# Issuing v and block 1's q first, and giving the last projection's halves a PSUM buffer each

## Chip, cores and metric

The kernel runs on one core of one Trainium2 chip. The metric is the device time of one execution in microseconds, as the median of several runs. Engines are named as in the profile: PE (TensorE, with PEld for its weight loads), DVE (VectorE), ACT (ScalarE), POOL (GpSimd) and SP (SyncE, which only issues transfers here).

## What is computed

Chunk-selected attention followed by an RMS norm and a SwiGLU feed-forward network, all from float32 inputs to a float32 output of 3072 x 512:

```python
# q, k, v: (4 batches, 8 heads, 768 tokens, 64)
k_min, k_max = k_chunks.min(3), k_chunks.max(3)            # chunks of 32 tokens
ub  = sum(maximum(q * k_min, q * k_max), axis=-1)          # a bound per query and chunk
top = argsort(where(causal, ub, -1e9))[..., -6:]           # each query keeps 6 chunks
p   = softmax(where(selected & causal, q @ k.T / 8, -1e9))
x   = (p @ v).transpose(0, 2, 1, 3).reshape(3072, 512)
xn  = x / sqrt(mean(x * x) + 1e-6) * rms_g
out = (silu(xn @ w_gate) * (xn @ w_val)) @ w_out           # 512 -> 1536 -> 512
```

## The kernel before

**Tiling.** The 768 tokens of each batch are cut in three, which gives twelve blocks of 256 tokens, taken in the order of `ORDER`: (0,0), (1,0), (2,0), (3,0), then later parts of the batches. Below, block 0 is (0,0), block 1 is (1,0) and block 2 is (2,0). The heads go in two groups of four (`g` = 0, 1). For each block and group `job` transposes k and q on DVE (L636, `kT` and `qT`), makes bf16 copies of them (L643 on ACT, L644 on POOL), takes the chunks' minima and maxima (L651), builds the bound's operands (`BO`, L676), computes the bound on PE (`upper`, L540 for the first part of a batch), picks the six chunks on DVE, computes the scores (L760, with the mask added by L771), their exponentials (`pt`, L810 on ACT), the triangle (L780 on POOL), the product with v (`values`, L836), and the division by the sums (`rden` L851, `xnat` L855). `norm` scales the rows (`junk` L872, `ri_all` L878 and L880, `xs` L906) and turns them (L916 on PE, `xsT` L929 on DVE). `ffn` does the feed-forward part: gate and value products (L960), tanh (`th`, L967), `tg` (L971), a copy of the value product (`vs`, L979), `hh` (L982 or L975), the projection (L1007), its scaling (`osb`, L1022 on ACT, L1025 on DVE) and the store (L1029).

**Order.** Every engine's order is written out. `Plan.run` walks the table `STEPS`: an entry of zero or more is an operation's number times 8 plus the engine (0 PE, 1 ACT, 2 DVE, 3 POOL, 4 SP); a negative entry is a fill, so many matmuls of `ident` (128 columns wide, or 512) into a PSUM buffer of pool `F`, whose result nobody reads (`keep_busy`, L1074). `SLOTS` holds, in the same order, which buffer of its pool each operation takes. Engines run their own lists in order and wait for one another by semaphores.

**PSUM.** Pool `F` has four buffers of one bank (128 x 512 float32) for everything but the scores; pool `S` has two of two banks each.

**Loads.** q and k of a block come in four transfers of 128 KB for the first three blocks (`load_qk`, L376 by `dma`), issued by SP; block 0's alternate between SP and ACT. v (`load_v`, two halves of 128 tokens, into `VX`) and the weights (`wg`, `wv`, `wo`, in thirds) are converted to bf16 on the way and are issued by POOL, on a queue of their own. Each half of v needs its column of ones (`ones`, L423) first. POOL also clears the buffers `BO` and `BD` (L420, L417) and makes `ident`. By `HELD` the first load of block 2 waits for the second third of `wg`, and that of block 3 for the first third of `wo`.

**Buffers of completions.** The transfers of SP and ACT report on eight semaphores in turn, so that the ninth transfer is issued when the first has landed, and so on.

**The end.** The last 128 tokens (`i, s` = 11, 1) are projected in two halves of 256 columns (`wide = 2`), named 11.1a and 11.1b, each in a first part of ten products (`project11.1a`) and a last part of two (`project11.1a+`). Both halves lie in one buffer of `F`. The order at the end on PE is 11.0, 11.1a, 11.0+, 11.1a+, 11.1b, 11.1b+; ACT scales half a (`out11.1a`) after 11.1b in the order, and half b after 11.1b+.

Of the kernel before, what the change touches and what calls it, by code (L numbers as in the profile page):

```python
# [11 lines left out]
ACT = mybir.ActivationFunctionType  # L12
# [21 lines left out]
class Plan:  # L34
# [13 lines left out]
        123, 228, 233, 155, 3, 99, 249, 244, 27, 257, 276, 83, 34, 203, 139, 281, 67, 268, 107, 315,  # L48
        131, 75, 115, 291, 380, 396, 323, 412, 538, 428, 466, 299, 404, 473, 482, 420, 443, 490,
        436, 545, 42, 307, 388, 498, 522, 506, 515, 179, 594, 529, 611, -2624, -320, 616, 562, 601,  # L50
        672, 554, 626, 571, 681, 50, 578, 457, 786, 587, 634, -82, -82, 792, 642, 689, 650, 57, 848,
        699, 802, 810, 9, 818, 857, 658, 826, 865, 834, 1098, 665, 875, 841, -176, 704, 451, 1042,
        -112, 736, 912, 713, 1114, 1107, 721, 1058, 1185, -146, 880, 1049, 1066, 19, 731, 1660, 746,
        331, 922, 889, 1130, 1628, 897, 754, 1075, 1644, 930, 1684, -274, -114, 1248, 1170, 961,
        760, 1676, 1082, 1091, 907, 195, 936, 1257, 1362, 1668, -80, 1192, 1138, 971, 1177, 1636,
        1202, 1147, 977, 1210, 770, 1154, 1163, 778, 1123, 1265, 946, -112, 984, 1652, 954, 1368,
        1218, 1001, 994, 1275, 1424, 1226, 1433, -51, 1312, 1378, 8384, 1011, 1234, 1441, 1322,
        1242, 1386, 8344, 1330, 147, 1451, 1017, 1394, 1402, 339, 1280, 1410, 8369, 1418, 1024,
        1289, 347, 1488, 8336, 1498, 1297, 1034, 355, 8401, 1506, 1456, 8353, 1307, 8480, 8410,
        1537, 363, 8362, 1336, 8497, 8488, 1547, 1346, 1762, 1473, 8528, 8506, 1465, 1851, 8513,  # L60
        1354, 1483, 1778, 8536, 8545, 8379, 1553, 1706, 1512, 8561, 8392, 1522, 371, 1530, 1834,
        1560, 1577, 8523, 8432, 1570, 8417, 8554, 1587, 8696, 8449, 1722, 8571, 8688, 8458, 8721,
        1730, 1593, 8584, 8705, 1802, 1739, 171, 2001, 1747, 1600, 8714, 1755, 8576, 8609, 1610,
        1841, 8731, 1856, 8440, 1713, 2212, 1866, 8427, 1794, 2228, 8736, 8593, 1874, 2260, 1811,
        8465, 1771, 2268, 8602, 8784, 2276, 1882, 2244, 1890, 8792, 1818, 1827, 1898, 8475, 8801,
        1906, 8753, 8832, 8817, 1699, 8762, 1912, 2220, 8810, 8849, 8619, 2008, 2308, 1921, 8744,
        2236, 2018, 1691, 1937, 2026, 2252, 2034, 8624, 8769, 2042, 8858, 1931, 1785, 2050, 8779,
        2284, 2057, 2324, 8888, 2292, 2354, 3050, 2064, 2363, 2300, 8632, 1947, 2073, 2316, 2370,
        8656, 2347, 2332, 2378, 2089, 2868, 2426, 2083, 8913, 2804, 8641, 2387, 2820, 2450, 2099,
        1952, 2844, 2442, 8827, -51, 2104, 8664, 2828, 1962, 2410, 8880, 2852, 8673, 2459, 2114,  # L70
        2395, 2900, 1970, 2417, 2403, 1976, 2122, 2836, 8840, 8897, 2482, 2884, 1986, 8928, 8906,
        8865, 2466, 2475, 2499, 3611, 2507, 1994, 8923, 2128, 8945, 2512, 2924, 2138, 2146, 2153,
        2916, 8875, 2161, 2860, 8936, 2522, 3476, 8954, 2171, 8976, 2812, 2530, 2538, 8684, 2946,
        2177, 3508, 2546, 8961, 2186, 2908, 2554, 8971, 2892, 2962, 2561, 2192, 2876, 2986, 9008,
        2433, 3484, 2339, 2201, 3010, 3524, 3532, 2491, 3034, 3540, 3019, 2970, 2568, 3492, 3003,
        3066, 8984, 2577, 9136, 3083, 8994, 2593, 2587, 3026, 9040, 4148, 9153, 3516, 2603, 2656,
        3116, 9162, 9057, 2979, 3043, 9048, 4283, 2953, 3500, 9066, 2665, 9004, 3058, 9096, 3075,
        4212, 9073, 2675, 3108, 9088, 3618, 2681, 163, 9083, 4252, 9121, 3634, 9144, 3092, 9105,
        3642, 2691, 3100, 9240, 9114, 9169, 3588, 2608, 9131, 9016, 9265, 3556, 2618, 2626, 2696,
        4164, 9025, 2632, 2706, 2714, 2720, 9179, 4236, 9184, 2730, 2745, 3572, 2642, 2650, 4220,  # L80
        2738, 3131, 9232, 9201, 3682, 4228, 3123, 2753, 9192, 4180, 9210, 211, 9249, 4244, 3706,
        2763, 3136, 9217, 9258, 2777, 9227, 9280, 3146, 3596, 2769, 5596, 3625, 9275, 9288, 3154,
        3658, 3564, 2993, 3580, 3162, 2784, 3675, 9313, 3548, 9328, 3691, 2793, 4196, 3722, 2931,
        4260, 4172, 9297, 3170, 4204, 9400, 9306, 4268, 4860, 3178, 9496, 9323, 9425, 9036, 3738,
        3185, 4156, 9392, 3698, 3651, 4188, 3755, 9336, 4290, 9409, 3603, 3764, 3192, 4330, 9521,
        3780, 9488, 3747, 9418, 3201, 3772, 3715, 4402, 9435, 9345, 9440, 4306, 3217, 9360, 3730,
        4347, 4417, 3788, 4339, 9457, 4354, 4876, 9505, 3667, 9466, 8652, 3211, 3232, 4378, 4452,
        2939, 9514, 4884, 9536, 3241, 5532, 4314, 3227, 4444, 9448, 3803, 9553, 4428, 3249, 3795,
        9562, 9544, 4868, 4370, 9473, 3304, 1620, 9569, 4386, 4322, 3808, 4436, 4394, 3313, 9579,
        4916, 3329, 9592, 4908, 3818, 9483, 4892, 4297, 9368, 4924, 3826, 9617, 3834, 3344, 3323,  # L90
        4940, 9377, 4980, 3339, 3256, 3353, 4972, 3842, 3280, 4900, 9584, 4459, 3290, 3361, 4932,
        3266, 3850, 9531, 9632, 3274, 9601, 3298, 3857, 3368, 9610, 5548, 3392, 3378, 9649, 4956,
        9627, 9640, 3386, 3402, 4964, 3417, 3410, 3864, 5580, 9658, 4275, 3425, 5644, 9680, 5002,
        3873, 9356, 4363, 5106, 4948, 3889, 3435, 5564, 5066, 9665, 9388, 3458, 3904, 4465, 5628,
        3442, 9675, 5612, 9712, 3913, 5018, 3883, 3452, 5026, 3899, 3921, 5090, 3468, 5042, 3976,
        5082, 4472, 5059, 3985, 5604, 5122, 5035, 4411, 4001, 9688, 4482, 3995, 9720, 9697, 5139,
        4016, 4490, 4498, 5049, 4011, 5148, 3928, 9729, 6308, 3952, 4025, 3938, 6356, 5098, 9792,
        3962, 4506, 5172, 4033, 9840, 3970, 5156, 3946, 9809, 4514, 5164, 4040, 9865, 9800, 9818,
        5620, 4521, 6332, 4050, 5714, 9832, 5572, 5114, 5588, 4592, 9849, 5179, 5652, 4058, 4064,
        5636, 5187, 4601, 9826, 9928, 6316, 5011, 4074, 9858, 4089, 5540, 187, 5075, 9880, 4082,  # L100
        6244, 4609, 5723, 6340, 5192, 6364, 4097, 6292, 9953, 4528, 4107, 5202, 9897, 9920, 4537,
        9906, 6324, 4114, 9752, 9937, 5556, 4130, 4547, 4553, 4124, 9968, 5730, 9777, 9946, 4563,
        4568, 9985, 4140, 5786, 9875, 5129, 9976, 5674, 4577, 91, 6260, 9994, 9888, 5803, 4585,
        6426, 4995, 5812, 9744, 9914, 6284, 4616, 10002, 6276, 9761, 5738, 4640, 9740, 5820, 4626,
        9770, 4664, 6268, 6442, 10072, 4673, 5690, 6348, 6980, 4634, 10256, 4689, 4683, 5210, 7628,
        5218, 5747, 10089, 7020, 10080, 10281, 219, 9963, 4650, 4704, 10098, 4658, 4987, 10120,
        6300, 4713, 6252, 5226, 10208, 7036, 10105, 5754, 5795, 5828, 10137, 10160, 4721, 9787,
        10146, 10168, 6506, 5698, 4728, 6521, 5234, 10177, 5707, 6540, 10008, 5683, 10193, 5762,
        7644, 10115, 5241, 6386, 7028, 10186, 5836, 10225, 4737, 6402, 6548, 10248, 10203, 6450,
        7676, 10128, 4745, 10234, 6988, 6371, 9708, 6410, 10016, 5771, 6916, 10296, 6490, 4699,  # L110
        10025, 7636, 10265, 5248, 6532, 10154, 10313, 4776, 6556, 10274, 5257, 6466, 6996, 4752,
        5273, 5267, 6948, 6474, 10304, 5843, 6956, 4762, 4770, 10036, 5667, 5288, 10322, 4786,
        10216, 5778, 5851, 5297, 7755, 7652, 4794, 10040, 4801, 7660, 10330, 6419, 4809, 5283, 7004,
        10242, 7012, 5305, 6483, 6435, 6498, 4819, 5856, 6457, 10291, 5360, 5866, 7692, 10048, 7724,
        5369, 4826, 5312, 6932, 5336, 5385, 6940, 5379, 10336, 6964, 5346, 5322, 10057, 5874, 5395,
        5330, 7684, 6569, 5882, 5659, 4836, 5400, 6562, 4842, 6576, 5409, 5354, 4852, 5890, 10368,
        5417, 5898, 7732, 6586, 6513, 7098, 5906, 10344, 7115, 6924, 5424, 7708, 10354, 5448, 7740,
        5912, 5434, 5458, 10068, 7058, 10376, 7748, 5921, 5442, 7067, 10496, 6594, 10364, 6602,
# [987 lines left out]
```

## Time and profile before

| | |
|---|---|
| median of 3 runs | 293.91 us (293.29 to 295.49) |
| the profiled execution's own time | 293.79 us |
| span of its profile | 292.1 us |
| PE, DVE, ACT, POOL busy | 279.0, 215.7, 207.1, 167.8 us |
| granted TensorE clock | 1.00 |

The span runs from the first to the last instruction of the profiled execution; the 1.7 us between it and that execution's time lie outside. PE's busy time includes the fills, so 96% doesn't mean that PE has useful work all the time. A row of the timeline gives the start, the length, the engine, the line, the operation, the tiles, the count, and in brackets the idle time before it with what ended it.

### The profile page before, as it was taken

The page shows a single profiled execution, that of the slowest core. Times are in us where ns is not written, and L with a number is a line of the kernel's source. Part 1 is how long each engine was busy: PE and PEld are TensorE (multiplying, and loading weights), DVE is VectorE, ACT ScalarE, POOL GpSimd, SP SyncE. Part 2 cuts the span into 40 slices and gives each one's busy share as a digit, 9 for nine tenths or more (in the row PEclk, how much of TensorE's full clock was granted, in tenths as well). Part 3 has the DMA queues.
Part 4 walks back from the last instruction along what each step waited for, and adds up shares of the span by engine and source line. Part 5 has one row for each costly group of instructions (what it writes and reads, how often), then busy time and mean ns, then how long its engine had stood idle before and what let it go on. Part 6 is the DMA issues. An engine that isn't in the chain of part 4 may idle for free.

```text
span 292.1 us, 11448 instructions
## 1 busy us (share of the span) xinstructions
PE 279.0 (96%) x4718; PEld 214.8 (74%) x4746; DVE 215.7 (74%) x626; ACT 207.1 (71%) x355; POOL 167.8 (57%) x268
## 2 busy tenths in 40 slices
PE   7979999999999899999999999999999999999994
PEld 7637887668877757888676786688678967688663
DVE  3778887889898799799989999987564715374240
ACT  2958887678888898877876595877679766564421
POOL 9649789879888785567683385427125116113410
PEclk9999999999999999999999999999999999999999
DMA  7999999988589584459599816912012300311022
GB/s 177 210 193 224 204 207 134 168 132 127 115 159 159 133 161 87 106 102 168 99 187 139 147 31 92 122 11 74 0 43 69 21 2 3 110 45 30 2 108 72
DMA packets 86388, 31.94 MB, mean 109 GB/s; under 512 B 74816, under 2 KB 81728, under 8 KB 86336
## 3 DMA queue, kind: packets, MB, share of 16 engines
q1 hardware_dynamic: 55776, 22.82, 33.9%
q0 software_dynamic: 29712, 7.87, 27.1%
q10 hardware_dynamic: 848, 0.53, 0.9%
q8 instruction: 37, 0.61, 0.9%
q14 instruction: 15, 0.12, 0.1%
HBM read 28.58 MB, written 6.29 MB: 119 GB/s over the span
## 4 chain that ended last, share of the span: by engine, by line
PE 84%; DMA 7%; DVE 5%; issue 2%; ACT 1%; DVEq 0%; SPq 0%
PE F L960 43%; PE F L1007 19%; PE S L760 7%; PE F L836 7%; DMA kraw<-in_k_dram 6%; PE S L771 3%; PE F L522 3%; DMA xsT<-xs 1%; PE F L540 1%; DVE kx L651 1%; DVE kT L636 1%; DVE xnat L855 1%; PE F L916 1%; DVE xs L890 1%; DVE tg L971 0%
## 5 line engine op out<-in xcount | busy, mean ns | idle before, releaser
L810 ACT ACTIVATE pt<-S 128x1024 bf16<-128x1024 f32 (+3 forms) x104 | 85.5, 858 | 29.7 <-PE S L771 26.4
L982 POOL TENSOR_TENSOR hh<-tg,vs 128x512 bf16<-128x512 bf16 x48 | 55.5, 1165 | 46.4 <-DVE tg L971 29.1
L960 PE MATMUL F<-xsT,wg 128*128 128x256 bf16 (+1 forms) x640 | 72.4, 262 | 0.2 <-DMA xsT<-xs 0.2
L960 PE MATMUL F<-xsT,wv 128*128 128x256 bf16 (+1 forms) x640 | 71.8, 262 | 0.6 <-issue 0.5
L1007 PE MATMUL F<-wo,hh 128*128 128x512 bf16 (+1 forms) x272 | 65.7, 370 | 2.3 <-issue 0.6
L971 DVE SCALAR_TENSOR_TENSOR tg<-th,F 128x512 bf16<-128x512 bf16 x72 | 48.3, 678 | 25.9 <-ACT th L967 19.6
L960 PEld LDWEIGHTS <-wg 128*128 128x128 bf16 x640 | 55.9, 98 | 9.2 <-issue 0.9
L960 PEld LDWEIGHTS <-wv 128*128 128x128 bf16 x640 | 56.2, 98 | 8.5 <-issue 1.0
L967 ACT ACTIVATE th<-F 128x512 bf16<-128x512 f32 x72 | 42.5, 599 | 13.9 <-PE F L960 12.6
L780 POOL TENSOR_SCALAR_AFFINE_SELECT pt<-pt 128x512 bf16<-128x512 bf16 x48 | 31.6, 665 | 27.9 <-ACT pt L810 27.7
L1007 PEld LDWEIGHTS <-hh 128*128 128x128 bf16 x300 | 27.5, 98 | 25.8 <-issue 1.0
L979 ACT ACTIVATE vs<-F 128x512 bf16<-128x512 f32 x48 | 28.5, 599 | 9.8 <-PE F L960 6.5
L760 PE MATMUL S<-qb,kb 32*128 32x256 bf16 (+1 forms) x800 | 32.8, 253 | 0.3
L651 DVE TENSOR_REDUCE kx<-kT 128x16 f32<-128x512 f32 x48 | 31.1, 669 | 0.2
L836 PE MATMUL F<-VX,pt 128*128 128x65 bf16 x672 | 27.5, 194 | 2.9 <-DMA VX<-in_v_dram 1.7
L836 PEld LDWEIGHTS <-pt 128*128 128x128 bf16 x672 | 25.4, 98 | 6.5 <-issue 3.3
L975 DVE TENSOR_TENSOR hh<-tg,F 128x512 bf16<-128x512 bf16 x24 | 16.1, 681 | 10.3 <-PE F L960 10.0
L760 PEld LDWEIGHTS <-kb 32*128 32x128 bf16 x800 | 13.6, 92 | 13.1 <-issue 11.6
L376 POOL DMA_DIRECT2D VX<-in_v_dram x24 | 22.7, 947 | 0.0
L771 PE MATMUL S<-mtd,chunkrow 32*128 32x128 bf16 (+2 forms) x384 | 20.3, 203 | 0.7 <-DVE xnat L855 0.7
L855 DVE TENSOR_TENSOR xnat<-F,rden 128x256 bf16<-128x256 f32 x48 | 19.5, 415 | 0.7
L771 PE MATMUL S<-mto,chunkrow 32*128 32x128 bf16 (+2 forms) x384 | 19.9, 203 | 0.0
(73 smaller groups left out, 337.3 us busy)
## 6 DMA issues: line engine op xcount, KB each, us to landing
out_dram<-osb SPq DMA_DIRECT2D x23, 256.0 KB, 3.0
kraw<-in_k_dram SPq DMA_DIRECT2D x72, 64.0 KB, 3.3
qraw<-in_q_dram SPq DMA_DIRECT2D x72, 64.0 KB, 3.1
VX<-in_v_dram POOLq DMA_DIRECT2D x24, 128.0 KB, 5.1
QX<-qT SPq DMA_DIRECT2D x32, 64.0 KB, 2.4
wv<-in_moe_w_val_dram POOLq DMA_DIRECT2D x3, 512.0 KB, 8.5
wg<-in_moe_w_gate_dram POOLq DMA_DIRECT2D x3, 512.0 KB, 13.5
wo<-in_moe_w_out_dram POOLq DMA_DIRECT2D x3, 512.0 KB, 10.2
```

The costliest lines, as they stand in the source:

```text
L651: plan.op(f"ext{n}{J}", "DVE", 0.585, 0.67, lambda n=n, op=op: VE.tensor_reduce(out=at(kx)[:, g, n], in_=at(kT).rearrange("p h (j c x) -> ...
L760: TE.matmul(s[a // 2][:, a % 2, c0:c0 + q1 - q0], kbt[r, t, ks], qbt[r, t, q0:q1], start=(t == 0), stop=(t == 1 and not mask), skip_group_ ...
L771: TE.matmul(o, chunkrow[r, BLK * kg + P * e:BLK * kg + P * (e + 1)], mv, start=False, stop=(d == 1), skip_group_check=True)
L780: GE.affine_select(out=d, in_=d, compare_op=ALU.is_ge, fill=0.0, base=0, pattern=[[0, 4], [1, P]], channel_multiplier=-1)
L810: lambda pt=pt, hs=hs, c0=c0, c1=c1, x=sc[hp]: SE.activation(out=at(pt)[:, hs, c0:c1], in_=at(x)[:, :, c0:c1], func=ACT.Exp, scale=SCALE), ...
L836: TE.matmul(o[:, a, :], p_[:, a, off:off + P], vt[:, e, 4 * g + a, :], start=(kb_ == 0 and a == 0), stop=(kb_ == nkb - 1 and a == 3), skip ...
L960: TE.matmul(at(p_)[:, n * W:(n + 1) * W], w[:, g, ht * P:(ht + 1) * P], at(xT)[:, g, x0:x0 + W], start=(g == 0), stop=(g == NP - 1), skip_ ...
L967: plan.op(f"tanh{U}.{hp}", "ACT", 0.48, 0.6, lambda th=th, gp=gp: SE.activation(out=at(th), in_=at(gp), func=ACT.Tanh, scale=0.5), pri - 0 ...
L971: VE.scalar_tensor_tensor(out=at(tg), in0=at(th), scalar=1.0, in1=at(gp), op0=ALU.add, op1=ALU.mult), pri - 30, reads=[th, gp], writes=[tg ...
L979: plan.op(f"vcopy{U}.{hp}", "ACT", 0.48, 0.6, lambda vs=vs, vp=vp: SE.activation(out=at(vs), in_=at(vp), func=ACT.Copy), pri + 0.1, reads= ...
L982: plan.op(f"hh{U}.{hp}", "POOL", 1.11, 1.16, lambda tg=tg, vs=vs, hh=hh: GE.tensor_tensor(out=at(hh), in0=at(tg), in1=at(vs), op=ALU.mult) ...
L1007: TE.matmul(at(op)[:, cs], at(key)[:, o:o + P], wo[:, ht, cs], start=(ht == 0), stop=(ht == NHT - 1), skip_group_check=True)
```

## The change

Three things are edited.

1. `dma` may put block 1's q and k on SP or ACT, as block 0's, and the order is written anew for the head of the kernel. Decoded from the tables:

| engine | before | after |
|---|---|---|
| POOL | BO03, ones3, eps, BO00, ident, BD02, ones9, ones1, BD00, BO01, **wv0**, ones0, BD01, BO02, **v000**, **wg1**, **v001**, v100, wg0 | ones0, BO03, ones3, eps, BO00, ident, **v000**, **v001**, BD02, ones9, BD00, BO01, BD01, BO02, ones1, **wv0**, **wg1**, v100, wg0 |
| SP | four of block 0, k1000, k1010, q1000, q1010, k1030, q1020, q1030, k1020 | four of block 0, q1000, q1020, k1000, k1010, k1030, k1020 |
| ACT | four of block 0, then computing | four of block 0, **q1010**, **q1030**, then computing |

Here v000 and v001 are the halves of block 0's v, wv0 and wg1 are thirds of weights, and q1000 to q1030 are block 1's q. After these the order of every engine's operations is the same as before; DVE's is unchanged from start to end.

2. PE's order of operations is unchanged, but its fills are sized anew: the first from 82 to 74 of 128 columns, and of the wide ones 5 to 4 and 3 to 2 ahead of `values(0, 0, 0)0`, 4 to 5 behind `values(0, 0, 1)0`, one more ahead of `values(1, 0, 1)1`, and one less ahead of `values(2, 0, 1)0`.

3. In `ffn`, the key of the projection's buffer now includes the half, so 11.1a and 11.1b take a buffer each.

```diff
-                dma(f"load {nm}{b}{m}{a}{k_}", ("SP", "ACT") if i == 0 else ("SP",), sv, dst, packets, cost,
+                dma(f"load {nm}{b}{m}{a}{k_}", ("SP", "ACT") if i < 2 else ("SP",), sv, dst, packets, cost,
...
                 tag = f"{i}.{s}" + ("ab"[x] if wide > 1 else "")
+                op = ("op", i, s, x)
...
                 o = plan.op(f"project{tag}", "PE", 0.216 * last / wide, 0.216 * last / wide + 0.17,
                             lambda project=project: project(0, last), pri,
-                            reads=hhs + [("wo", y) for y in range(3)] + ([op] if x else []),
-                            writes=[done, op] if not x else [done], takes=[] if x else [(op, "F")])
+                            reads=hhs + [("wo", y) for y in range(3)],
+                            writes=[done, op], takes=[(op, "F")])
```

The first lines of the table that changed:

```diff
     STEPS = (
-        123, 228, 233, 155, 3, 99, 249, 244, 27, 257, 276, 83, 34, 203, 139, 281, 67, 268, 107, 315,
+        131, 228, 233, 123, 155, 3, 99, 249, 244, 27, 257, 276, 291, 34, 281, 268, 299, 83, 412,
...
```

`SLOTS` changes with it. Compared by who held a buffer of `F` before, five operations differ besides the last projection: `wv(0, (1,)).4` now follows `wv(0, (1,)).0` in its buffer (before: `wg(0, (1,)).0`), `values(1, 0, 1)1` follows `wg(0, (1,)).0`, `wv(0, (0,)).4` follows `values(1, 0, 0)1`, `turn(1, (1,))` follows `wv(1, (0,)).0`, and `wg(0, (1,)).8` follows `wg(0, (0,)).8`. From there on each operation follows the same one as before. 11.1b takes the buffer that held `wg(11, (0, 1)).10`.

186 rows, old and new, of tables (SLOTS, STEPS) are left out of this document.

## The prediction

> **What bounds the kernel now.** I read the page, then the chain of waits, then the timeline engine by engine at the two ends, where the change lies. The page first:
>
> ```profile
> span 292.1 us, 11448 instructions
> PE 279.0 (96%) x4718; PEld 214.8 (74%) x4746; DVE 215.7 (74%) x626; ACT 207.1 (71%) x355; POOL 167.8 (57%) x268
> PE 84%; DMA 7%; DVE 5%; issue 2%; ACT 1%; DVEq 0%; SPq 0%
> ```
>
> PE sets the pace, except for the DMA and DVE shares of the chain. The chain in order of time shows where most of those lie (start, length, what):
>
> ```profile
> 0.80 3.05 DMA kraw<-in_k_dram
> 3.87 5.78 DMA kraw<-in_k_dram
> 9.67 7.49 DMA kraw<-in_k_dram
> ...
> 25.43 1.79 PE F L960 x32
> ```
>
> The first 17.2 us are three transfers of k in a row: the first of block 0 lands at 3.85, and only then is the first of block 1 issued; that lands at 9.65, and only then is the last of block 1, which lands at 17.16. From 25.43 on, where the feed-forward products begin, the chain is nearly all PE. So a gain in the head counts if it reaches 25.43, and one in the tail counts in full. DVE and PE in the head (timeline; brackets give the idle time before):
>
> ```profile
> 13.16 0.24 DVE L591 STREAM_TRANSPOSE mtd<-mk 128x64 bf16<-128x64 bf16 x1
> 16.27 0.71 DVE L636 STREAM_TRANSPOSE qT<-qraw 128x512 f32<-128x512 f32 x1 [2.87 <-DMA qraw<-in_q_dram]
> 17.24 1.31 DVE L636 STREAM_TRANSPOSE kT<-kraw 128x512 f32<-128x512 f32 x2 [0.25 <-DMA kraw<-in_k_dram]
> 13.86 0.82 PE L1074 MATMUL F<-ident 128*128 128x512 bf16 x3
> 16.41 0.42 PE L836 MATMUL F<-VX,pt 128*128 128x65 bf16 x8 [1.73 <-DMA VX<-in_v_dram]
> 16.67 1.02 PE L1074 MATMUL F<-ident 128*128 128x512 bf16 x4
> 17.63 0.29 PE L760 MATMUL S<-qb,kb 32*128 32x128 bf16 x8
> 18.05 2.55 PE L1074 MATMUL F<-ident 128*128 128x512 bf16 x11
> 20.54 0.29 PE L760 MATMUL S<-qb,kb 32*128 32x128 bf16 x8
> 21.84 0.44 PE L540 MATMUL F<-qT,BO 64*64 64x32 f32 x16
> ```
>
> DVE is done with block 0's selection at 13.40 and stands still until block 1's q (16.2) and k (17.2). PE waits for v till 16.41, but that wait is not on the chain: behind it PE still runs 11 fills that cost nobody anything.
>
> **Part 1, the loads.** *v.* POOL's list holds the same instructions, reordered, so it ends as before; v's first half is issued at about 2.0 instead of 4.34, its second by 2.9.
>
> ```profile
> 2.79 0.97 POOL L376 DMA_DIRECT2D wv<-in_moe_w_val_dram  x1
> DMA to landing us min/median/max: 8.3/8.5/11.8
> 4.34 0.91 POOL L376 DMA_DIRECT2D VX<-in_v_dram  x1
> 5.97 1.79 POOL L376 DMA_DIRECT2D VX<-in_v_dram  x2
> DMA to landing us min/median/max: 12.0/13.1/14.0
> 5.23 0.77 POOL L376 DMA_DIRECT2D wg<-in_moe_w_gate_dram  x1
> DMA to landing us min/median/max: 6.6/13.5/16.0
> ```
>
> The landing rows are, in turn, those of the `wv` loads, of the v loads up to 26 us, and of the `wg` loads. v's first half landed at 4.34 + 12.0 = 16.3, behind wv0 in POOL's queue. With nothing ahead of it, it lands well before PE asks at about 14.3. That removes the 1.73 us, but alone is worth nothing, since the next thing late is block 1's k on DVE.
>
> *q and k.* SP's eight block-1 loads landed from 9.65 to 17.16, which is 7.51 / 7 = 1.07 us a load on one queue. The change leaves SP six of them; two q go to ACT's queue. At the same pace SP's sixth, the last k, lands at 9.65 + 5 x 1.07 = 15.0. I take 15.3, as q's four on two queues will slow one another a little and v's small packets lie beside them. Bounds: 15.0, and 17.16 if the two queues share one flow. q is all down by then (before 13.4 at that pace), so DVE turns it in its idle time and then waits for k alone: the start of `kT` moves from 17.24 to 15.3, a gain of **1.9** (0 to 2.2).
>
> *ACT pays the issues* of two q loads, and each waits for a completion to reuse:
>
> ```profile
> 2.69 1.28 ACT L643 ACT_TABLE_LOAD   x1 [2.69 <-issue]
> 6.43 2.09 ACT L643 ACTIVATE kb<-kT 128x512 bf16<-128x512 f32 x2 [2.46 <-DVE kT L636]
> 8.82 2.10 ACT L643 ACTIVATE qb<-qT 128x512 bf16<-128x512 f32 x2 [0.30 <-DVE qT L636]
> 4.91 0.79 SPq L376 DMA_DIRECT2D qraw<-in_q_dram  x2
> ```
>
> The ninth and tenth issues on SP went out from 3.87, the eleventh (third completion) at 4.91. By the same completions ACT's second q goes out at 4.91, ends 0.4 later at 5.3, and the table load behind it ends at 6.6. `kb` starts 0.2 late, and the 0.30 us ahead of `qb` swallow it: **0**. Without that cover it would cost 0.2 on a path that has until 15.3 anyway.
>
> *Can PE follow?* From 13.86: two fills (0.22 each) to 14.30, `values` 0.26 (16.41 to 16.67) to 14.56, five fills at 0.24 to 15.76, scores 0.42 (17.63 to 18.05) to 16.18, eleven fills at 0.217 to 18.57, then the same 1.30 as before (20.54 to 21.84) to `upper` of block 1 at 19.8 to 19.9. That is 2.0 ahead of 21.84, so PE admits the 1.9. The 8 short fills less at the start lie ahead of a bound that waits for DVE and POOL: **0**.
>
> *What is late next.* Block 2's loads wait for `wg`'s second third, which now has v's second half ahead of it:
>
> ```profile
> 18.73 0.31 SPq L376 DMA_DIRECT2D qraw<-in_q_dram  x1
> L376 SPq DMA_DIRECT2D qraw<-in_q_dram x4: 312/495/1407, 18.7 to 22.0; - x4
> DMA to landing us min/median/max: 5.9/7.2/7.5
> 31.77 0.71 DVE L636 STREAM_TRANSPOSE qT<-qraw 128x512 f32<-128x512 f32 x1
> ```
>
> `wg`'s third landed at 5.23 + 13.5 = 18.73, and SP's first load of block 2 went out at that moment. q of block 2 was down at 22.0 + 7.5 = 29.5 at the latest, and DVE took it at 31.77; moved by 1.9 it asks at 29.9. A v half costs POOL's queue up to 1.2 us where no loads run beside it (v's second, issued at 5.97, was down by 5.97 + 14.0 = 20.0 at the latest, 1.2 after `wg`), and the queue starts 0.8 earlier (v at 2.0, wv0 was at 2.79). So I put `wg` at 19.1 and q at 29.9: no slack left, **+0.2** for what I may have missed (0 to 2.2).
>
> **Part 2, buffers and fills.** `wv(0, (1,)).4` takes the buffer that ACT's copy `vs` frees, no longer the one that DVE's `tg` frees:
>
> ```profile
> 32.41 0.65 DVE L971 SCALAR_TENSOR_TENSOR tg<-th,F 128x512 bf16<-128x512 bf16 x1
> 32.76 0.62 ACT L979 ACTIVATE vs<-F 128x512 bf16<-128x512 f32 x1
> 33.15 1.06 PE L960 MATMUL F<-xsT,wv 128*128 128x128 bf16 x16
> ```
>
> `tg` ended at 33.06, ahead of 33.15; `vs` ends at 33.38, so PE waits until about 33.44: **+0.3** if ACT and PE move together (bounds 0 and 0.3). The fill added behind it costs 0.22 on a PE that is otherwise full there; the fill removed ahead of `values(2, 0, 1)0` gives at most the same back. I take **+0.2** (0 to 0.22).
>
> **Part 3, the last projection.**
>
> ```profile
> 282.38 5.16 PE L1007 MATMUL F<-wo,hh 128*128 128x512 bf16 x33
> 287.57 0.38 ACT L1022 ACTIVATE osb<-F 128x256 f32<-128x256 f32 x1 [5.08 <-PE F L1007]
> 288.01 0.38 PE L1007 MATMUL F<-wo,hh 128*128 128x256 bf16 x2 [0.47 <-ACT osb L1022]
> 288.42 0.38 ACT L1022 ACTIVATE osb<-F 128x256 f32<-128x256 f32 x1 [0.47 <-PE F L1007]
> ```
>
> Half a's sums were complete before 11.1b began, yet ACT read them only at 287.57, when PE's 11.1b (282.38 + 5.16 = 287.54) let go of the shared buffer; then 11.1b+ waited 0.47 for ACT. With two buffers PE goes straight on. Products overlap: the eight at 16.41 end at 16.83, and the next began at 16.67, 0.16 inside. So 11.1b+ starts at 287.38 instead of 288.01, and ACT and the store behind it move along: **-0.63**. If sharing the buffer was not the reason, 0. The buffer that 11.1b takes held the last gate product, whose readers must be through before 11.0+ can run, and that stands ahead of 11.1b: no new wait.
>
> **Sum.** -1.9 + 0.2 + 0.3 + 0.2 - 0.63 = -1.83. On the profiled execution's 293.79 (span 292.1 and 1.7 outside it) that gives 291.96. The runs' median, 293.91, is 0.12 above it, so I forecast **292.1**, with 291.3 to 292.9 for this case alone.
>
> **Rivals.** *Two queues, one flow (0.20).* Block 1's k lands at 17.16 as before and the head gains nothing: +0.3 (or 0) and +0.2 (or 0) stand against -0.63, so 293.3 to 293.8, about **293.6**. For it: k's last transfer took 7.49 us though issued alone. Against it: block 0's eight loads, on two queues, were down between 3.85 and the 8.07 at which DVE started its `qT` below, 4.2 / 7 = 0.6 us a load against 1.07 on one.
>
> ```profile
> 8.07 0.71 DVE L636 STREAM_TRANSPOSE qT<-qraw 128x512 f32<-128x512 f32 x1 [0.16 <-DMA qraw<-in_q_dram]
> ```
>
> The Trainium skill, DMA: Bandwidth & Descriptors, section "Issuing engines are not separate DMA queues", speaks for this rival: transfers from several engines run on the same 16 DMA engines, and issuing on several saves only the issuing time. The same page's section "Queues, rings and completion order" has each DMA engine take turns among the queues with work, which beside POOL's weights would give two queues two shares of three. By the one 293.6, by the other 292.1; the 0.6 against 1.07 agrees with the second.
>
> *The weights come too late (0.17), slower.* v's second half goes ahead of `wg` while q and k are loading. Beside such loads a v half cost more: v's first landed at 16.3, wv0 at 2.79 + 8.3 = 11.1 (8.3 is the least of wv's landing times), so 5.2 us. Then `wg` lands at up to 18.73 + 5.2 - 0.8 = 23.1, block 2's q 10.8 (29.5 - 18.73) later at 33.9, and DVE and all behind it stand 2.1 us later than before. It turns slower once q is later than 31.9, `wg` later than 21.1. At `wg` = 22 q comes at 32.8: +1.0 + 0.5 - 0.63, about **294.8**; at worst 295.9. Against it: q and k now finish some 2 us sooner, and leave POOL's queue alone from then.
>
> *More than forecast (0.13).* k at 15.0, PE's limit of 2.0 used in full, no wait at `vs` and the fills even: -2.0 - 0.63 - 0.2 for the fill removed, 290.96 by the profiled execution and **291.1** as a median.
>
> **How the numbers follow.** Forecast 0.50, one flow 0.20, late weights 0.17, more 0.13. The range 290.7 to 294.8 takes in the first two, half of the third and most of the fourth. A measurement of this kernel tells about 1%, 2.9 us, from no change. Under 291.0 lie half of the last rival and a little of the forecast: 0.12. Over 296.8 lies nothing that I priced; I leave 0.06 for what I haven't seen. Within 1%: 0.82.
>
> **What would show it.** Right: `values` with no wait for `VX`; `kT` of block 1 waiting for `kraw` alone and starting near 15.3; the first L960 near 23.6 instead of 25.3; SP's first block-2 load near 19; 11.1b+ with no idle time for ACT. Wrong: `kT` near 17.2 (one flow); `qT` at 30 to 34 with a wait for `qraw` (late weights); ACT's `qb` later than 9.1; the head's gain there at 25 us and gone by 60, where a slack that I didn't look at would have run out.

## The result, and the profile after

The changed kernel takes **292.7 us** (median of 20 runs, 290.95 to 294.61), the kernel before on the same chip 294.49: a ratio of 0.9931, 95% interval 0.9908 to 0.9954. The forecast was 1.8 us less than before, and the medians differ by 1.8. The terms that were to make up this sum are another matter: the largest of them did not come true, and most of what follows is about that. All ratios below are to runs of the kernel before on the same chip, with 95% intervals.

From the page of the changed kernel: the span, PE's row, the queue that brings the engines their code (pieces, MB, share), and the chain by engine.

```profile
span 290.6 us, 11431 instructions
PE 279.8 (96%) x4709; PEld 215.1 (74%) x4737; DVE 215.5 (74%) x626; ACT 206.6 (71%) x355; POOL 167.8 (58%) x268
...
q8 instruction: 37, 0.61, 0.9%
...
PE 78%; DMA 8%; DVE 4%; SPq 3%; ACT 2%; issue 2%; ACTq 0%; DVEq 0%
```

The span is 1.5 us shorter. The chain in order of time now begins with q's load and then k's (start, length, what):

```profile
2.21 5.56 DMA qraw<-in_q_dram
8.14 8.52 DMA kraw<-in_k_dram
```

The last load of k is issued at 8.14 and lands 8.52 us later, at 16.66. Before, it landed at 17.16. The timeline of DVE shows block 1:

```profile
13.55 0.71 DVE L636 STREAM_TRANSPOSE qT<-qraw 128x512 f32<-128x512 f32 x1
16.78 1.31 DVE L636 STREAM_TRANSPOSE kT<-kraw 128x512 f32<-128x512 f32 x2 [2.51 <-DMA kraw<-in_k_dram]
```

q no longer keeps DVE waiting, but k does: `kT` starts at 16.78, only 0.46 ahead of before's 17.24. PE's timeline, in the head and around 29 us:

```profile
14.52 0.42 PE L836 MATMUL F<-VX,pt 128*128 128x65 bf16 x8
21.38 0.44 PE L540 MATMUL F<-qT,BO 64*64 64x32 f32 x16
24.80 1.05 PE L960 MATMUL F<-xsT,wg 128*128 128x128 bf16 x16
28.64 0.21 PE L760 MATMUL S<-qb,kb 32*128 32x128 bf16 x1
29.76 0.29 PE L760 MATMUL S<-qb,kb 32*128 32x128 bf16 x7 [0.91 <-issue]
```

The values product waits no more. `upper` of block 1 is 0.46 ahead (21.84 before), the first L960 0.47 (25.27). Then PE stands for 0.91 us in the middle of one group of score products, seven of whose eight matmuls have not run, and the profile names nothing that it waited for ("issue"). Behind that stop, and behind the buffer that now depends on ACT's `vs`, the gain is gone (timeline of all engines):

```profile
32.07 1.06 PE L960 MATMUL F<-xsT,wg 128*128 128x128 bf16 x16
32.22 0.65 DVE L971 SCALAR_TENSOR_TENSOR tg<-th,F 128x512 bf16<-128x512 bf16 x1
32.57 0.62 ACT L979 ACTIVATE vs<-F 128x512 bf16<-128x512 f32 x1
33.24 1.05 PE L960 MATMUL F<-xsT,wv 128*128 128x128 bf16 x16
```

`wv(0, (1,)).4` starts at 33.24, 0.09 later than before's 33.15: it comes 1.17 us behind the product ahead of it, where before it took 0.89. The end, on PE and ACT:

```profile
281.82 5.37 PE L1008 MATMUL F<-wo,hh 128*128 128x512 bf16 x35
285.92 0.39 ACT L1023 ACTIVATE osb<-F 128x256 f32<-128x256 f32 x1 [3.99 <-PE F L1008]
287.23 0.38 ACT L1023 ACTIVATE osb<-F 128x256 f32<-128x256 f32 x1 [0.93 <-PE F L1008]
```

All 35 products now run in one piece. From their start to ACT's last copy it takes 287.23 - 281.82 = 5.41 us; before, 288.42 - 282.38 = 6.04.

### The profile page after: what moved, and what is told of

It reads as the page before. It is cut to its first block, busy times and chain, and to the rows that moved or that the text cites. A ratio compares the mean times of both kernels' runs of the same rounds, so it can differ in the third digit from the quotient of the medians.

```text
span 290.6 us, 11431 instructions
## 1 busy us (share of the span) xinstructions
PE 279.8 (96%) x4709; PEld 215.1 (74%) x4737; DVE 215.5 (74%) x626; ACT 206.6 (71%) x355; POOL 167.8 (58%) x268
## 4 chain that ended last, share of the span: by engine, by line
PE 78%; DMA 8%; DVE 4%; SPq 3%; ACT 2%; issue 2%; ACTq 0%; DVEq 0%
PE F L960 39%; PE F L1008 19%; PE S L760 7%; PE F L836 6%; DMA kraw<-in_k_dram 3%; SPq L376 3%; DMA qraw<-in_q_dram 2%; PE S L771 2%; PE F L522 2%; DMA out_dram<-osb 2%; DMA xsT<-xs 1%; PE F L540 1%; DVE xnat L855 1%; PE F L916 1%; DVE kx L651 1%
## 5 line engine op out<-in xcount | busy, mean ns | idle before, releaser
L960 PE MATMUL F<-xsT,wg 128*128 128x256 bf16 (+1 forms) x640 | 72.4, 262 | 0.9 <-DVE tg L971 0.7
L960 PE MATMUL F<-xsT,wv 128*128 128x256 bf16 (+1 forms) x640 | 71.6, 262 | 0.2
L960 PEld LDWEIGHTS <-wg 128*128 128x128 bf16 x640 | 55.9, 98 | 9.8 <-issue 1.6
L960 PEld LDWEIGHTS <-wv 128*128 128x128 bf16 x640 | 56.2, 98 | 8.5 <-issue 0.8
L780 POOL TENSOR_SCALAR_AFFINE_SELECT pt<-pt 128x512 bf16<-128x512 bf16 x48 | 31.6, 665 | 27.4 <-ACT pt L810 27.3
L636 DVE STREAM_TRANSPOSE kT<-kraw 128x512 f32<-128x512 f32 x24 | 16.4, 694 | 6.0 <-DMA kraw<-in_k_dram 5.6
```

Source lines behind the costliest of these rows:

```text
L780: GE.affine_select(out=d, in_=d, compare_op=ALU.is_ge, fill=0.0, base=0, pattern=[[0, 4], [1, P]], channel_multiplier=-1)
L960: TE.matmul(at(p_)[:, n * W:(n + 1) * W], w[:, g, ht * P:(ht + 1) * P], at(xT)[:, g, x0:x0 + W], start=(g == 0), stop=(g == NP - 1), skip_ ...
```

## The experiments

**1. The tail alone.** The kernel before, with a buffer of its own for 11.1b. The order of every engine's operations is that of before. The line that makes the difference:

```diff
+                op = ("op", i, s, x)
```

> Only part 3: the kernel before, with a buffer of its own for the second half of the last projection. If the shared buffer is what held ACT's first copy (the prediction's step): that copy starts near 285.9 to 286.6 instead of 287.57, 11.1b+ has no idle time for ACT, and the last copy starts 0.63 us earlier than 288.42; ratio 0.998. If something else held it: 287.57 and 288.42 as before, ratio 1.000.

Ratio 0.9976 (0.9945 to 1.0007). PE and ACT at its end:

```profile
284.23 5.37 PE L1008 MATMUL F<-wo,hh 128*128 128x512 bf16 x35
289.64 0.38 ACT L1023 ACTIVATE osb<-F 128x256 f32<-128x256 f32 x1 [0.93 <-PE F L1008]
```

289.64 - 284.23 = 5.41 us again. The shared buffer was what held the end, and 0.63 us is its price. But this execution came to its last projection 1.85 us later than the profiled one of before (284.23 against 282.38), with a program that is the same up to there. Two executions of one kernel differ by more than what is looked for here, and experiment 7 shows one reason.

**2. q first, two loads on ACT; GpSimd's list as before.**

```diff
-SP:  k1000, k1010, q1000, q1010, k1030, q1020, q1030, k1020
+SP:  q1000, q1020, k1000, k1010, k1030, k1020     ACT: q1010, q1030
```

> Only the q and k part: the kernel before, with block 1's q first, two of its loads on ACT's queue, GpSimd's list as before. If each queue has a pace of its own (the prediction): SP's sixth load, the last k, lands near 15.3 and kT of block 1 starts there. If all queues share one flow: the same bytes stand ahead of the last k as before, kT starts near 17.2, and qT of block 1 no longer waits.

Ratio 0.9978 (0.9945 to 1.0011). DVE and PE:

```profile
17.39 1.30 DVE L636 STREAM_TRANSPOSE kT<-kraw 128x512 f32<-128x512 f32 x2 [3.45 <-DMA kraw<-in_k_dram]
16.40 0.44 PE L836 MATMUL F<-VX,pt 128*128 128x65 bf16 x8 [1.78 <-DMA VX<-in_v_dram]
26.44 1.05 PE L960 MATMUL F<-xsT,wg 128*128 128x128 bf16 x16
```

k comes at 17.39: two queues carry no more than one did. That is what one flow says, and the forecast's 15.3 falls. The first L960 is 1.17 late although `kT` is only 0.15 late. The reason stands in the stretches by time (PE, PEld, DVE, ACT and POOL busy, then the granted clock, DMA share, GB/s):

```profile
16.00:18.00 2.00, 1.60 (x12) 0.69 (x11) 0.61 (x1) 0.00 (x0) 0.96 (x2) 0.66 1.87 168
18.00:20.00 2.00, 2.00 (x37) 0.94 (x36) 2.00 (x7) 1.84 (x3) 0.05 (x1) 0.50 1.73 193
```

Behind a wait of 1.78 us for v, PE's clock was 0.50. In the profiled execution of before it stayed 1.00 behind a wait of 1.73.

**3. v and the constants first; q and k as before.**

```diff
-POOL: ..., ident, BD02, ones9, ones1, ..., wv0, ones0, ..., v000, wg1, v001
+POOL: ones0, ..., ident, v000, v001, BD02, ones9, ..., ones1, wv0, wg1
```

> Only GpSimd's part: v and the constants ahead of the weights, the loads of q and k as before. Both theories: the first values product no longer waits 1.73 us for VX, and this alone brings nothing, first L960 at 25.2 to 25.6. Own pace: kT of block 1 at 17.2 as before. One flow: the two v halves stand ahead of wv0 and only one of them did so before, kT at 17.2 to 18.

Ratio 1.0005 (0.9977 to 1.0032). The values product starts at 14.74 without a wait for v, `kT` at 16.83, the first L960 at 24.82. In the time of the run, v's wait alone is worth nothing, as forecast. In this execution PE also stands for 1.84 us from 28.77 to 30.61, and the granted clock is 0.50 from 31.32 to 34.73.

**4. The changed kernel with the weights issued later.**

```diff
-POOL: ..., ones1, wv0, wg1, v100, wg0, bd1, ones6, relu, ..., tri a, tri a, v101, half q, half, tri b, wv1, dk, bd1, tri b
+POOL: ..., ones1, bd1, ones6, relu, wg1, ..., tri a, wv0, tri a, v100, half q, half, tri b, wg0, dk, bd1, tri b, v101, wv1
```

> The changed kernel with wg's second third, wv's first, v's next half and wg's first third issued at 9.5 to 17 us instead of 6.1 to 8.5, so that GpSimd's queue is empty while block 1's q and k load. One flow: the last k lands near 14, kT of block 1 follows qT without a wait near 14.3, the first L960 starts at 23.0 to 23.8 instead of 24.8, and the time is 0.5 to 1.5 us under the changed kernel's. Own pace: kT at 16.8 as in the changed kernel, first L960 at 24.8 or later. In either case it is no gain if wg's second third lands after 23.

Ratio 0.9960 (0.9926 to 0.9994). DVE and PE, and the stretches behind:

```profile
14.79 1.29 DVE L636 STREAM_TRANSPOSE kT<-kraw 128x512 f32<-128x512 f32 x2
23.89 1.05 PE L960 MATMUL F<-xsT,wg 128*128 128x128 bf16 x16
29.69 0.29 PE L760 MATMUL S<-qb,kb 32*128 32x128 bf16 x7 [1.76 <-issue]
...
30.00:32.00 2.00, 2.00 (x30) 2.00 (x28) 0.07 (x1) 0.51 (x2) 0.00 (x0) 0.60 1.24 205
32.00:34.00 2.00, 2.00 (x24) 2.00 (x22) 1.98 (x5) 1.43 (x4) 1.05 (x3) 0.55 1.24 212
```

With only v's two halves on GpSimd's queue beside them and no weights, q and k come 2 us sooner on the same two queues: `kT` starts at 14.79, right behind `qT`. The flow is shared by all queues, GpSimd's among them. From 10 to 12 us all queues together moved 0.45 MB in the changed kernel and 0.44 MB here, but GpSimd's had 0.30 MB of it there and 0.01 MB here; q and k got the rest. PE follows (first L960 at 23.89), and then loses nearly all of it. The stop that took 0.91 us in the changed kernel takes 1.76 here and ends at 29.69, practically where it ended there (29.76), and the clock falls behind it. So something that the loads did not move fixes that moment.

**5. The changed kernel without its tail.**

```diff
-                op = ("op", i, s, x)
```

> The changed kernel without part 3: the loads, the buffers and the fills stay, the last projection shares one buffer again. Theory A: what the head gains is used up by 33 us, so the ratio is 0.999 to 1.001 and the whole of the change is the tail. Theory B: before, PE's wait of 1.73 us for v stands at the edge of a clock that halves (it was 1.78 in the run with q on ACT, and the clock was 0.50 behind it), so that many executions of before lose another 1.2 us that the profiled one doesn't show, and none does here: ratio 0.995 to 0.997.

Ratio 0.9982 (0.9958 to 1.0005), between the two theories, and the interval excludes neither. `kT` started at 17.23, the first L960 at 25.26, as before the change.

**6. The changed kernel with the buffers and fills of before.**

```diff
-PE: wv(0, (1,)).4 F0, fill, values(1, 0, 1)1 F2, wv(0, (0,)).4 F3, ...
+PE: wv(0, (1,)).4 F2, values(1, 0, 1)1 F3, wv(0, (0,)).4 F0, ...
```

> The changed kernel's loads and last projection with the buffers and fills of before. The prediction's step: wv(0, (1,)).4 no longer waits for ACT's vs, so it starts 0.89 us behind the product before it as it did before (32.26 to 33.15) and not 1.17 (32.07 to 33.24), 0.3 us gained there; the time 0 to 0.4 us under the changed kernel's. Rival: the gain meets a wait that comes anyway (PE without code, DVE's tg), and the time is the changed kernel's.

Ratio 0.9978 (0.9948 to 1.0008). PE's timeline at the two products:

```profile
31.74 1.06 PE L960 MATMUL F<-xsT,wg 128*128 128x128 bf16 x16
32.64 1.06 PE L960 MATMUL F<-xsT,wv 128*128 128x128 bf16 x16
```

They are 0.90 us apart instead of 1.17, so the wait for `vs` is real and costs 0.27. No gain in time shows. Soon after, this execution has a stop of 0.83 us, up to 36.1, that the changed kernel doesn't have, and both reach the transpose of block 1's second half (L916, about 39.5) together.

**7. PE's code cut elsewhere.** 8 more narrow fills at the start, and 14 wide fills as 28 narrow ones: 44 more PE instructions in about the same PE time.

```diff
-PE: 74 narrow, ..., 2 wide, ..., 2 wide, ..., 4 wide, ..., 2 wide, ..., 8 wide
+PE: 82 narrow, ..., 4 narrow, ..., 4 narrow, ..., 8 narrow, ..., 4 narrow, ..., 4 wide and 8 narrow
```

> The changed kernel with 8 more narrow fills at the start and 14 wide fills of the first 20 us as 28 narrow ones, which is 44 more PE instructions and about the same PE time. Theory C: PE stands still after its 960th recorded instruction because the next 256 instructions (16 KB) have not come; then the wait follows the count: behind the 960th again, which is now in the wg product 22 pairs ahead of the scores, and, since the dense stretch is cut more evenly, 0.2 to 0.6 us of it instead of 0.91, with up to 0.4 more behind the 704th. Rival: the scores wait for data or a buffer; then 0.9 us stay ahead of the same scores, whatever the count.

Ratio 0.9975 (0.9944 to 1.0005). The 0.91 us ahead of the scores are gone, so they were no wait for data. But theory C had a shorter stop behind the same count, and there is none. Another stop stands earlier:

```profile
15.56 0.29 PE L1075 MATMUL F<-ident 128*128 128x128 bf16 x2 [0.91 <-issue]
```

This is a fill in the middle of a row of fills, which reads only `ident`. How many instructions PE had run at its stops shows what they are. The stretches from 0 to a moment within three stops of experiment 1, whose head is that of before (in brackets the instructions, PE's first, then PEld's):

```profile
0.00:15.50 15.50, 13.22 (x222) 10.87 (x222) 9.34 (x30) 9.74 (x18) 11.64 (x33) 1.00 1.06 206
0.00:28.70 28.70, 25.23 (x477) 18.98 (x477) 20.80 (x73) 19.39 (x38) 22.03 (x55) 1.00 1.23 206
0.00:35.50 35.50, 31.15 (x605) 24.69 (x605) 26.28 (x84) 24.77 (x49) 27.00 (x62) 1.00 1.23 206
```

PE and PEld together: 444, 954, 1210 records. With the records of PE's sequencer, which the stretches leave out and the counts in the expectations take in, they are 449, 961 and 1217, which is 512 and 256 apart. The changed kernel, at its stop:

```profile
0.00:29.30 29.30, 25.61 (x477) 18.91 (x477) 20.43 (x73) 19.32 (x38) 22.23 (x55) 1.00 1.25 205
```

954 as well, although 18 instructions fewer lie ahead of the same scores. By the page, queue q8 of the kind "instruction" moves 37 pieces of 0.61 MB / 37 = 16 KB. The trace has 9493 records of PE, PEld and their sequencer, and 37 x 256 = 9472: this fits one piece for each 256 instructions of PE, at 64 bytes each. Packet by packet, the last piece ahead of this stop's end ran from 26.93 to 28.32, and PE went on at 29.76; in experiment 4 it ran from 27.13 to 28.44, with PE back at 29.69. In experiment 7 it ran from 25.80 to 27.00, PE came to the same count at 28.3, and there was no stop. So PE had run out of code; why the piece came sooner in experiment 7 stays open.

**8. Experiments 6 and 7 together.**

```diff
-PE: changed kernel's buffers and fills
+PE: before's buffers; 2, 2, 5 and 4 wide fills as twice as many narrow ones
```

> Both edits: the changed kernel's loads and last projection, before's buffers, and the fills split so that the code's pieces end 44 instructions sooner in the program. Theory C with the buffers' step: 0.3 us at wv(0, (1,)).4 and 0.3 to 0.6 at 29 us, 0.5 to 0.9 us under the changed kernel's time. Rival: later waits for code take both back, and the time is the changed kernel's within 0.4.

Ratio 0.9936 (0.9905 to 0.9968). Its stop, and the count there:

```profile
29.71 0.45 PE L960 MATMUL F<-xsT,wg 128*128 128x128 bf16 x5 [0.83 <-issue]
...
0.00:29.20 29.20, 24.32 (x477) 19.35 (x477) 19.89 (x72) 18.59 (x36) 21.52 (x54) 1.00 1.26 200
```

954 records again, and now the stop falls inside a product of `wg`, 44 instructions ahead of the score product at which the changed kernel stopped: it stayed with the count and not with the operation. Its length (0.83 us against 0.91) did not shrink as expected, and a further stop of 1.77 us stood behind the 444th. The time is the changed kernel's, as the rival had it.

**9. Before, with the wait for v filled.**

```diff
-PE: 3 wide fills, values(0, 0, 0)0
+PE: 11 wide fills, values(0, 0, 0)0
```

> The kernel before with 8 more wide fills (1.74 us) ahead of the first values product, so that PE does not stand still while v loads; loads, buffers and tail as before. Theory B: of the five idle stretches of 1.73 to 1.84 us seen in the head so far, three were followed by 4 us at half clock, which cost 1.2 us in the run with q on ACT; filling the one of before saves 0.5 to 0.7 us on the median, ratio 0.9975 to 0.9985, clock 1.00 from 14 to 20 us. Theory A: the wait costs nothing, ratio 1.000.

Ratio 1.0026 (0.9998 to 1.0053), against the 0.998 of theory B. PE was busy throughout at clock 1.00, values started at 16.72 and the first L960 at 25.41. So before did not lose what theory B supposed, or the fills cost as much where v comes early (`values` started at 14.86 in experiment 1).

**10. The changed kernel once more** (no edit).

> The changed kernel once more, for its own spread: block 1's kT has started at 16.72 to 17.40 in five executions with its loads, and at 16.21 and 17.24 in two with the old ones. If the loads gain nothing there, kT is in 16.7 to 17.4 again and the ratio is 0.993 to 0.997, of which the tail is 0.998.

Ratio 0.9948 (0.9915 to 0.9982), in the range expected; `kT` at 16.44, somewhat ahead of it, the first L960 at 24.46, the stop behind the 954th record 1.37 us long and over at 29.87.

**11. Late weights, old buffers, split fills, new tail.** GpSimd's order is that of experiment 4, PE's that of experiment 8.

```diff
-POOL: ones1, wv0, wg1, v100, wg0, bd1, ...
+POOL: ones1, bd1, ones6, relu, wg1, ..., tri a, wv0, tri a, v100, ..., wg0
```

> Old buffers, split fills, new tail, and the weights issued at 9.5 to 17 us: what the runs so far speak for, together. kT of block 1 starts near 14.8 (one flow), the first L960 near 23.9. Theory C: the wait for code behind the 960th PE instruction then ends 5.7 to 6.7 us after the 704th, near 28.5 to 29.5, so 0.3 to 1.0 us of the head's gain lives on, ratio 0.990 to 0.993. Rival: the wait lasts past 1.7 us, the clock halves behind it, and the gain is gone: 0.994 or more.

Ratio 0.9960 (0.9926 to 0.9994). DVE and PE:

```profile
15.05 1.30 DVE L636 STREAM_TRANSPOSE kT<-kraw 128x512 f32<-128x512 f32 x2 [0.75 <-DMA kraw<-in_k_dram]
23.78 1.05 PE L960 MATMUL F<-xsT,wg 128*128 128x128 bf16 x16
29.18 0.45 PE L960 MATMUL F<-xsT,wg 128*128 128x128 bf16 x5 [1.95 <-issue]
39.30 0.39 PE L916 MATMUL F<-ident,xs 128*128 128x128 bf16 x4
```

The head is 1.5 us ahead of before at 23.78, waits 1.95 us for code, and starts the L916 at 39.30 (39.18 before). From there on this execution has 0.53 us of stops up to the last projection, before has 1.50, so that the projection starts at 280.84, 1.54 ahead of before's. The ratio is the rival's. In the profiled execution the clock that the rival named stayed at 1.00 behind the 1.95 us, but that one, with 291.30 us, was the second shortest of twelve. The mean granted clock of each execution was taken as well, and 3.41 us at half clock take 0.006 off it: ten of the twelve had 0.994 or less. So in most of them the clock did fall somewhere, as the rival said; where, the profile of one execution can't show.

**12. Before, with v's second half ahead of its first.**

```diff
-POOL: ..., BO02, v000, wg1, v001
+POOL: ..., BO02, v001, v000, wg1
```

> The kernel before with v's second half issued ahead of its first, so that the first values product waits about 1.2 us longer, 2.4 to 3.2 us. Behind it stand 11 fills (2.4 us). Theory A: the longer wait is hidden as the 1.73 us were, first L960 at 25.3 to 26.0, ratio 1.000 to 1.002. Theory B: the clock falls to 0.50 from 16.5 to 20 us, the scores and fills behind it take twice as long, first L960 at 26.4 or later, ratio 1.003 to 1.006.

Ratio 1.0050 (1.0023 to 1.0078), which is theory B's. PE, and one of the two stretches with a low clock:

```profile
17.55 0.42 PE L836 MATMUL F<-VX,pt 128*128 128x65 bf16 x8 [2.39 <-DMA VX<-in_v_dram]
19.84 3.45 PE L1074 MATMUL F<-ident 128*128 128x512 bf16 x11
27.60 1.05 PE L960 MATMUL F<-xsT,wg 128*128 128x128 bf16 x16
...
18.00:20.00 2.00, 2.00 (x37) 0.95 (x36) 2.00 (x4) 1.14 (x2) 1.48 (x4) 0.57 1.69 181
```

A wait 0.66 us longer than before's 1.73 puts the first L960 2.33 later, of which `kT`, 0.49 later itself, explains little. The eleven fills that were to hide it took 3.45 us instead of 2.55. Eight of the ten executions had a mean clock of 0.994 or less; of before's 103 beside the experiments 16 had. A late start is carried on, too, where an early one isn't: the L916 that starts at 39.18 before starts at 41.45 here.

## Why the prediction was right, and where it was wrong

The number held, 1.8 us forecast and 1.8 between the medians. But of the sum -1.9 + 0.2 + 0.3 + 0.2 - 0.63 the traces show only the last three terms, which come to about -0.1. The first, which was to be the gain, was not found, so as far as the runs tell the total came out right by luck. One execution each of kernels with the old loads and with the new (left out: those that take one part of the loads alone, move the weights or lengthen v's wait; us; the idle time is the sum of PE's stops over 0.3 us between 25 us and the last projection):

| kernel | kT of block 1 | first L960 | idle in stops | last projection starts |
|---|---|---|---|---|
| before | 17.24 | 25.27 | 2.18 | 282.38 |
| 1, tail | 16.21 | 24.25 | 4.74 | 284.23 |
| 9, wait filled | 17.38 | 25.41 | 3.93 | 284.53 |
| changed | 16.78 | 24.80 | 1.62 | 281.82 |
| 5, no tail | 17.23 | 25.26 | 2.78 | 283.18 |
| 6, old buffers | 16.72 | 24.74 | 2.46 | 283.04 |
| 7, code split | 17.03 | 25.06 | 2.30 | 281.98 |
| 8, both | 17.40 | 25.43 | 3.91 | 283.88 |
| 10, changed again | 16.44 | 24.46 | 3.46 | 282.77 |

**v first: right.** The wait is gone and brought nothing by itself (experiments 3 and 9). The reason given, fills behind it that cost nobody anything, was too simple. They are a cover only at full clock, and experiment 12 shows what comes when the wait is longer.

**q and k: wrong, and the largest term.** "At the same pace SP's sixth, the last k, lands" took 1.07 us a load for the pace of SP's queue. It is the pace of a flow that all queues share. `kT` starts at 16.94 on the mean of the three rows with old loads and at 16.93 on that of the six with new ones, the first L960 at 24.98 and 24.96: in place of -1.9 the means show 0, where single executions of either kind spread over 1.0 to 1.2 us. Experiment 2 has the same bytes ahead of k on two queues and the same time, and experiments 4 and 11 keep the weights off GpSimd's queue and have k 2 us sooner. "Two queues, one flow", given 0.20, was right for this step. What spoke against it, 0.6 us a load in block 0, was measured while GpSimd's loads had hardly begun: by 6 us in before's trace the queues of SP and ACT had moved 1.0 MB, which is nearly all of block 0's q and k, and GpSimd's 0.03 MB. The section "Issuing engines are not separate DMA queues" of the Trainium skill's DMA: Bandwidth & Descriptors, set against that 0.6, was the better guide; experiment 2's 17.39 agrees with it.

**What the chain allowed: wrong.** "A gain in the head counts if it reaches 25.43" held in no profiled execution. Experiments 1, 4, 10 and 11 and the changed kernel were 0.5 to 1.5 us ahead at the first L960; at the L916 that starts at 39.18 before, all were 0.1 us or more behind it. The stop for code ended at 29.18, 29.87 and 29.76, with PE there at 27.23, 28.50 and 28.85 (experiments 11 and 10, and the changed kernel). Had k landed at 15.3, as it nearly did in experiment 11 (`kT` at 15.05), most of the gain would have ended there.

**ACT's issues: right in the sum.** `kb` was 0.49 late instead of 0.2, `qb` 0.22 (9.04, under the 9.1 set as a limit), and PE's first stop of over 0.3 us behind them is the one for code. **Late weights: the +0.2 did not come.** SP's first load of block 2 went out at 18.76 (18.73 before, 19.1 forecast), and DVE took that q at 31.6 without a wait.

**Buffers and fills: right in place and size.** The wait for `vs` is 0.27 to 0.28 us (0.3 forecast), and the fill added behind it runs from 34.13 until `values` starts at 34.34, 0.21 us (0.2 forecast; what the fill removed later gives back was not followed). But they cost no time that the runs can tell: experiment 6 takes both away, and its profiled execution is no earlier at the L916 (39.48 against 39.41).

**Tail: right**, 6.04 to 5.41 us in the changed kernel and in experiment 1, which is the 0.63 forecast.

**What stays open.** The profiled pair differs by 0.56 us where the last projection starts, and by as much in the idle column: the two are even but for their stops. The medians' 1.8 is more than the tail's 0.63, which alone would be a ratio of 0.9979, outside the 0.9908 to 0.9954 of the first measurement and inside the 0.9915 to 0.9982 of the second (experiment 10). The two halves of the change measured alone give 0.9976 x 0.9982 = 0.9958, some 1.2 us, each with an interval of 0.3% on both sides. The granted clock, which theory B of experiment 5 had as the cause, doesn't explain the rest: a mean clock of 0.994 or less came in 16 of 103 executions of before beside the experiments and in 6 of 30 of the changed kernel, and those without it still differ by 2.0 us (medians 294.64 and 292.63). Whether the new loads make the stops shorter by 0.6 to 1 us on the mean, or the spread did this, nine profiled executions with 1.6 to 4.7 us in stops can't tell. None of the versions was measurably faster than the changed kernel.

## What to carry to other kernels

Before a second queue is credited with a gain, look whether the loads that it would pass share the flow with something else: keeping the weights off the other queue moved k by 2 us here, splitting k's own queue by nothing. A gain that is read from a chain must also be followed through the places where the profile says "issue"; a stop that ends at nearly the same time however early the engine comes swallows most of what was gained ahead of it. Where two executions of the same program differ by 2 us, take the place-by-place differences from several traces, and believe those that repeat, as the 0.63 at the end did.

## What the runs showed of the hardware

**Code arrives in pieces, and PE can outrun it.** Between 12 and 43 us, all of PE's stops of over 0.3 us in the fourteen traces but the waits for v and one of 0.47 in experiment 5 (for ACT's `pt`) stand behind the 449th, 961st, 1217th or 1473rd record, the sequencer's included. These lie 512, 256 and 256 apart, and the operation there differs. The profile put them down to "issue", to DVE's `xnat` (before), to DVE's `tg` (experiment 1) or to ACT's `th` (experiment 9), depending on what else ended shortly ahead. PE went on 1.2 to 1.6 us after the piece had landed. The 256 records ahead of the 954th (without the sequencer's) are 4.6 to 4.7 us of PE work; where PE stopped behind them, it went on 5.6 to 6.8 us after it had begun them. What sets that time was not tried.

**PE's clock halves behind some short waits.** It fell to 0.50 for 3.41 us behind idle stretches of 1.76, 1.78, 1.84 and 2.39 us (experiments 4, 2, 3, 12), and stayed at 1.00 behind 1.73, 1.77 and 1.95 (before, 8, 11). The Trainium skill's TensorE: Matmul & The Clock Gate, section "What's actually happening", has the clock set by a free-running window of about 3.4 us and halved after an idle one. The traces agree with the window: their records of full clock last whole multiples of 3.41 us, 3 (10.24), 7 (23.89) or 84 (286.72). They differ on how idle it has to be. With the windows laid back from these changes, the four stretches that halved the clock put all of their 1.76 to 2.39 us into one window; of the three others a boundary cut off a part and left 1.54, 1.42 and 1.75 us in one. So here 1.76 us of idle in a window were enough and 1.75 were not, a little over half of it, and where the window's edge falls decides what a wait of that length costs.
